# Attention and a squared-ReLU MLP on one core: earlier loads of the second batch, another conversion schedule, ReLU in place in PSUM

## Chip, core and metric

The kernel runs on one core of one Trainium2 chip. A core has TensorE (PE, with its weight loads as PEld), VectorE (DVE), ScalarE (ACT), GpSimd (POOL) and SyncE (SP), an on-chip memory SBUF, the matmul result memory PSUM, and DMA engines that move data between device memory and SBUF. The metric is the device time of one execution in microseconds (us); lower is better.

## The reference

```
kv  = einsum('bhsd,bhse->bhde', k, v)          # b=8, h=8, s=576, d=64
out = einsum('bhsd,bhde->bhse', q, kv)
out = out / sqrt(mean(out*out, -1) + 1e-6) * g_norm
x   = out as (b*s, h*d)                        # 4608 x 512
h   = x @ w_in                                 # 512 x 2048
r   = maximum(h, 0);  g = r * r
y   = g @ w_out                                # 2048 x 512
```

q, k, v and g_norm are float32. w_in and w_out come as float64 and are turned into float32 on the chip; the result is float32.

## The kernel before

The 4608 tokens are nine strips of 512. For each strip the kernel makes x from the attention, then the up products (x @ w_in, ReLU, square) and the down products (@ w_out). Strip 0 multiplies w_in plainly: 16 products (`up_first`, L741), each of a 128-column block of w_in with all 512 tokens, in four accumulating matmuls into one PSUM bank of 512 columns. Its down products, and the later strips, use sums and differences of blocks so that seven products do the work of eight; those of w_out are made on the chip and stored in device memory (`w_out`, `w_deep`).

**Opening.** Attention works on pairs of heads. For the pairs 0 to 3 of batch 0 a hand-written list of steps (L619 to L624) alternates the transposed query, k times v, the query product and the norm with the first conversions and up products. k and v of the last 64 tokens of each head (the "rests", k_rest and v_rest) are separate tiles; each pair's k times v ends with matmuls that read them (L408). The gain g_norm goes into the tile g_col, which scales x on its way out of PSUM (L545).

**Conversions.** The weights come as 32 pieces of 512 KiB (`raw`, 8 buffers): 16 of w_in and then 16 of w_out. A piece costs two ScalarE activations (L242, L245) and four VectorE instructions (L254 to L263). `convert(n)` (L319) does conversions, of two pieces each, until n are done; ScalarE always works two pieces ahead. Conversions 2 to 7 are of w_in, 8 to 11 of w_out's first half, 12 to 15 (`sums_out`, L300) of its second half, with four subtractions more each per piece; these also store their result (tile `wt`) to `w_out` with four DMAs each (L313). After each conversion the next pieces' loads are issued; each waits until the conversion of the piece eight before it has freed the buffer. The steps of strip 0 call `convert` by their number i: behind steps 0 to 3 up to 3, 4, 5 and 7, ahead of steps 4 to 10 up to 8, 9, 10, 10, 11, 12, 13, and behind steps 11 to 15 up to 13, 14, 15, 16, 16. So three conversions stand between the ReLU of product 3 and that of product 4.

**ReLU and square.** After each product of strip 0 ScalarE takes two halves of 256 tokens from PSUM: ReLU from PSUM into the tile `gt` in SBUF (L756), then the square in place there (L757). Four banks rotate, so product i waits for the ReLUs of product i-4.

**Queues.** Every engine executes its instructions in the order in which the program issues them. Nearly all loads and stores are issued by SyncE, in program order; a DMA that has to wait holds up all behind it. Eight semaphores tell of landed DMAs in rotation, so a DMA also waits until the one eight places before it (SyncE and ScalarE counted together) has landed. ScalarE issues the rests of batch 0 and g_col. The attention of batch 1 runs between the last products of strip 0 and in its down steps. Its loads are issued ahead of steps 4, 6 and 8 (pairs 0, 1, 2; `load_next`), 5 (rests) and 15 (the "last queries": the last 64 queries of each head of batches 0 and 1, tile q_rest); pair 3 and batch 2 follow from `key_value`.

**After the up steps.** VectorE makes `g_s` (sums of `gt`, L735), then sums of w_out's blocks into tiles `w_t` (`store_deep_sums`, L825). These tiles lie where the conversion buffers were, so the first waits for the last stores of `wt`. The norm's result x_n of the next strip comes behind them on VectorE, and TensorE's transposes of it (xt_ps, L570) stand between two down products. SyncE then stores the `w_t` sums (L837), stores converted blocks of w_out from w_in's tile to device memory (L863) and reads back weight blocks (`w_blk`, L804). `sums_in` (L287) then writes sums of w_in's blocks over the stored ones and so waits for those stores.

Of the kernel before, what the change touches and what calls it, by code (L numbers as in the profile page):

```python
# [14 lines left out]
AF = mybir.ActivationFunctionType  # L15
# [5 lines left out]
def kernel(  # L21
# [34 lines left out]
    nc = tc.nc  # L56
# [14 lines left out]
    TH = STRIP // 2  # L71
# [77 lines left out]
    def load_rest(b, eng):  # L149
        h = b % 2  # L150
        half = slice(REST * h, REST * (h + 1))
        for t, src in ((k_rest[half], k), (v_rest[half], v)):
            eng.dma_start(out=t, in_=src[b, :, C * P : S].rearrange("h s d -> s h d"))

    def load_q_rest(b, eng, one=None):
        h = b % 2
        if h == 0 and not one:
            q_rest[b // 2] = rest_pool.tile([P, H, D], FP32, name="q_rest", tag="q_rest")
        src = q[b, :, C * P : S]
        if b < Q_ON_PE:  # L160
            eng.dma_start(out=q_rest[b // 2][REST * h : REST * (h + 1)], in_=src.rearrange("h s d -> s h d"))
            return
        t = squares(q_rest[b // 2])
        for a in range(4) if one is None else (one,):
            hq, f = divmod(a * SQ, D)
            for kq in range(2):
                eng.dma_start(
                    out=t[ts(a, SQ), 2 * h + kq], in_=src[hq::2, ts(kq, SQ), f : f + SQ].rearrange("p i f -> i p f")
                )
# [4 lines left out]
    def load_next(q_eng=nc.sync, names="kvq"):  # L174
        u = next(to_load, None)
        if u is not None:
            load(*u, q_eng, names)
# [141 lines left out]
    def convert(n):  # L319
        while converted[0] < min(n, len(conversions)):  # L320
            fn, a = conversions[converted[0]]
            fn(a)
            converted[0] += 1
# [9 lines left out]
    nc.scalar.sqrt(one, one)  # L333

    load_next()
    load_rest(0, nc.scalar)
    for p in range(1, NP):
        load_next()
        load_piece()
# [2 lines left out]
    g_src = g_norm.rearrange("(d u) -> d u", u=1)  # L342
    for h in range(2):
        nc.scalar.dma_start(out=g_col[ts(h, D)], in_=g_src)


    qT, kvd, x_n, xt = {}, {}, {}, {}
# [319 lines left out]
    def attend(n):  # L667
        while slice_at[0] < min(n, len(slices)):
            fn, a = slices[slice_at[0]]
            fn(*a)  # L670
            slice_at[0] += 1
# [53 lines left out]
    def quarters(s, g):  # L725

        if (s, 11) not in gq:
            for q in (11, 12, 21, 22):
                gq[s, q] = g_pool.tile([P, FQ, TH], FP32, name="gt", tag="gt")
        return {q: gq[s, q][:, 2 * g : 2 * g + 2, :] for q in (11, 12, 21, 22)}  # L730

    def sum_g1(s, g):
        dest = quarters(s, g)
        s1 = gq[s, 1, g] = sum_pool.tile([P, 2, TH], FP32, name="g_s1", tag="sum")
        nc.vector.tensor_tensor(out=s1, in0=dest[12], in1=dest[22], op=ALU.add)  # L735
# [5 lines left out]
    def up_first(g, fh, i):  # L741

        tag = TAG_UP[2 * fh + i]
        if g == 0 and 2 * fh + i in first_sums:
            ps = first_sums.pop(2 * fh + i)
        else:
            ps = fpsum.tile([P, STRIP], FP32, name=f"ps_{tag}", tag="f")
            for kc in range(NP):
                nc.tensor.matmul(
                    ps, lhsT=w_in[:, kc % KH, g, kc // KH * 2 + fh, ts(i, P)], rhs=xt[0][:, :, kc, :],  # L750
                    start=kc == 0, stop=kc == NP - 1,
                )
        dest = quarters(0, g)
        for th in range(2):
            o = dest[(11, 12, 21, 22)[2 * fh + th]][:, i, :]
            nc.scalar.activation(o, ps[:, ts(th, TH)], AF.Relu)  # L756
            nc.scalar.activation(o, o, AF.Square)  # L757

    def up(s, g, p):
        open_bank(p)  # L760
# [406 lines left out]
    for s in range(N_STRIP):  # L1167
        attend(ready[s])
        if s == DEEP_UP - 1:
            while queried:  # L1170
                attend(slice_at[0] + 1)
            psums.close()
            fpsum = ctx.enter_context(tc.tile_pool(name="fpsum", bufs=5, space=bass.MemoryType.PSUM, reuse_waits="tile"))
            apsum = ctx.enter_context(tc.tile_pool(name="apsum", bufs=1, space=bass.MemoryType.PSUM, reuse_waits="tile"))
        if s >= DEEP_UP:
            steps = [(0.5, up_slot, (s, slot)) for slot in range(55)]
        elif s == 0:
            steps = [(2, up_first, (g, fh, i)) for g in range(NG) for fh in range(2) for i in range(2)]
        else:
            steps = [(1, up, (s, g, p)) for g in range(NG) for p in ORDER]  # L1180
        n_up = len(steps)
        if s < DEEP:

            steps += [(2, down, (s, p, i)) for p in (ORDER if s else (1, 2, 5, 6, 7, 3, 4)) for i in range(2)]
        else:
            steps += [(2, down_deep, (s, k, i)) for k in range(7) for i in range(2)]
        goal, begun = ready.get(s + 1, len(slices)), slice_at[0]
        if s >= DEEP_UP:
            goal = max(goal, min(ready[DEEP_UP] + (len(slices) - ready[DEEP_UP]) * (s - 1) // (N_STRIP - DEEP_UP - 1), len(slices)))
        total, done = sum(w for w, _, _ in steps), 0  # L1190
        for i, (w, fn, a) in enumerate(steps):
            if s == 0 and i < n_up:

                if 4 <= i < 11:
                    convert(5 + (3 * i + 2) // 4)
                if i in (4, 6, 8):
                    load_next()
                if i == 5:
                    load_rest(1, nc.sync)
                if i == 15:  # L1200
                    for b in range(2):
                        load_q_rest(b, nc.sync)
            elif s == 0 and i == n_up:
                convert(len(conversions))
                conv.close()

                stream_pool = ctx.enter_context(tc.tile_pool(name="stream", bufs=4, reuse_waits="tile"))
                sum_pool = ctx.enter_context(tc.tile_pool(name="sum", bufs=8, reuse_waits="tile"))
            if s == 0 and n_up <= i < n_up + 2:
                for g in range(2 * (i - n_up), 2 * (i - n_up) + 2):  # L1210
                    sum_g1(0, g)
            if s == 0 and n_up + 2 <= i < n_up + 4:
                for g in range(2 * (i - n_up) - 4, 2 * (i - n_up) - 2):
                    sum_g3(0, g)
            fn(*a)
            if s == 0 and i < 4:

                convert((3, 4, 5, 7)[i])
            done += w
            if s:  # L1220
                clock[0] += 3.2 if i >= n_up else 2.2 if s == DEEP else 1.2
                soon = tiles_due and tiles_due[0][2][0] // NT == s + 1
                if i == n_up + 10:
                    while tiles_due and tiles_due[0][2][0] // NT == s + 1:
                        _, f, a = tiles_due.popleft()
                        f(*a)
                elif not due(keys_due) and not (soon and due(tiles_due)):
                    least = 2.1 if s == DEEP else 4.5 if i < n_up else 3.3
                    if not (n_up * 2 // 3 < i < n_up + 3) and clock[0] >= dripped[0] + least:
                        dripped[0] = clock[0]  # L1230
                        drip(True)
                pace = 25 if s == DEEP else 36
                attend(begun + (goal - begun) * min(i + 1, pace) // pace)
                if s == DEEP and i == n_up - 3:
                    leaf_sums(s, 4)
                if s == 1 and i in range(2, 23, 3):
                    deep_sums_in((1, 6, 5, 4, 0, 2, 3)[i // 3])
                if s == 1 and i in (21, 22, 23, 25):
                    stream()
                continue  # L1240
            if i == n_up + 1:
                stream()
            if i == n_up + 8:
                load_next()
            if i == n_up + 9:
                load_rest(2, nc.sync)
                load_q_rest(2, nc.sync)
            if i - n_up in (7, 8, 9, 12):
                sums_in((7, 8, 9, 12).index(i - n_up))
            if i == n_up + 11:  # L1250
                sums_x(1)
            n = i + 1 - (n_up - 6)
            pairs, m = divmod(max(n - 2 * NP, 0), 3)
            attend(min(ready[0] + min(max(n, 0), 2 * NP) + (n >= 2 * NP) + 4 * pairs + (0, 2, 2)[m], goal))
            if 11 <= i < n_up:

                convert(5 + (3 * i + 2) // 4)
# [30 lines left out]
```

## Time and profile before

| what | us |
|---|---|
| three runs | 915.65, 916.85, 921.91 |
| median | 916.85 |
| profiled execution | 920.21 |
| its span, first to last instruction | 918.0 |
| TensorE busy | 888.5 (97%) |
| VectorE busy | 731.3 (80%) |
| ScalarE busy | 318.3 (35%) |
| GpSimd busy | 305.8 (33%) |

The profile is one execution. Its times count from the first instruction; "[2.12 <-ACT gt L756]" behind a row says that the engine stood idle for 2.12 us and that a ScalarE instruction of line 756 ended this. "SPq" and "ACTq" are issues of DMAs. The granted clock is the share of its full rate that TensorE was allowed. The page's row of the DMA engines by 40 slices and that of TensorE's clock read:

```
PEclk8999999999999999999999999999999999999999
DMA  9699898898989697979886987888657866785385
```

Up to about 92 us strip 0's opening and up products run, from there to 156 us its down products, and from then on the strips 1 to 8.

### The profile page before, as it was taken

The page shows a single profiled execution, that of the slowest core. Times are in us where ns is not written, and L with a number is a line of the kernel's source. Part 1 is how long each engine was busy: PE and PEld are TensorE (multiplying, and loading weights), DVE is VectorE, ACT ScalarE, POOL GpSimd, SP SyncE. Part 2 cuts the span into 40 slices and gives each one's busy share as a digit, 9 for nine tenths or more (in the row PEclk, how much of TensorE's full clock was granted, in tenths as well). Part 3 has the DMA queues.
Part 4 walks back from the last instruction along what each step waited for, and adds up shares of the span by engine and source line. Part 5 has one row for each costly group of instructions (what it writes and reads, how often), then busy time and mean ns, then how long its engine had stood idle before and what let it go on. Part 6 is the DMA issues. An engine that isn't in the chain of part 4 may idle for free.

```text
span 918.0 us, 20609 instructions
## 1 busy us (share of the span) xinstructions
PE 888.5 (97%) x8246; PEld 825.8 (90%) x8246; DVE 731.3 (80%) x1256; ACT 318.3 (35%) x638; POOL 305.8 (33%) x315
## 2 busy tenths in 40 slices
PE   7899998999999999999999999999999999999998
PEld 6434777889899999999999998999999999999998
DVE  2999878678958895789688967887689868975886
ACT  4797450321023701370128011720263027201710
POOL 0000000930057604560456044513362246234700
PEclk8999999999999999999999999999999999999999
DMA  9699898898989697979886987888657866785385
GB/s 266 222 292 307 252 341 269 247 293 309 285 265 239 229 341 238 252 238 337 268 220 217 333 286 206 241 283 305 207 163 256 304 220 186 255 304 177 124 310 184
DMA packets 172367, 235.71 MB, mean 257 GB/s; under 512 B 83568, under 2 KB 137328, under 8 KB 163824
## 3 DMA queue, kind: packets, MB, share of 16 engines
q1 hardware_dynamic: 171056, 234.14, 80.0%
q8 instruction: 65, 1.06, 0.5%
q10 hardware_dynamic: 1216, 0.26, 0.2%
q14 instruction: 30, 0.25, 0.1%
HBM read 197.66 MB, written 36.70 MB: 255 GB/s over the span
## 4 chain that ended last, share of the span: by engine, by line
PE 72%; DVE 11%; DMA 9%; ACT 3%; issue 2%; SPq 2%; DVEq 0%; ACTq 0%
PE ps_B L929 20%; PE ps_A L1117 16%; PE ps_A L929 15%; PE ps_B L1117 8%; PE ps_C L1117 4%; PE ps_A L708 4%; DMA q<-in_q_dram 2%; PE kv_ps L408 2%; PE x_ps L442 1%; PE ps_B L708 1%; DMA w_out<-w_in 1%; DMA w_blk<-w_out 1%; DVE w_c L260 1%; DVE w_t L280 1%; DVE o_sb L944 1%
## 5 line engine op out<-in xcount | busy, mean ns | idle before, releaser
L929 PE MATMUL ps_B<-w_blk,g_s 128*128 128x128 f32 x1024 | 126.2, 275 | 0.0
L929 PEld LDWEIGHTS ps_B<-w_blk,g_s 128*128 128x128 f32 x1024 | 120.0, 192 | 0.2
L1117 PE MATMUL ps_A<-x_l,w_in 128*128 128x128 f32 x784 | 104.1, 276 | 0.0
L929 PE MATMUL ps_B<-w_blk,gt 128*128 128x128 f32 x768 | 97.5, 275 | 2.0 <-DMA w_blk<-w_out 1.1
L280 POOL TENSOR_TENSOR x_l<-xT 128x256 f32<-128x256 f32 x21 | 16.1, 768 | 247.7 <-PE ps_A L929 247.7
L1117 PEld LDWEIGHTS ps_A<-x_l,w_in 128*128 128x128 f32 x784 | 95.4, 192 | 0.5 <-DVE gt L1129 0.2
L929 PEld LDWEIGHTS ps_B<-w_blk,gt 128*128 128x128 f32 x768 | 91.5, 192 | 2.4 <-issue 1.3
L929 PE MATMUL ps_A<-w_blk,g_s 128*128 128x128 f32 x768 | 93.6, 275 | 0.0
L929 PEld LDWEIGHTS ps_A<-w_blk,g_s 128*128 128x128 f32 x768 | 89.6, 192 | 0.0
L1129 POOL TENSOR_TENSOR snap<-snap,gt 128x512 f32<-128x512 f32 x35 | 46.5, 1330 | 123.2 <-ACT snap L1134 53.4
L1134 ACT COPY snap<-ps_A 128x512 f32<-128x512 f32 x63 | 36.6, 582 | 132.6 <-PE ps_A L1117 123.0
L944 DVE TENSOR_TENSOR o_sb<-o_sb,ps_B 128x256 f32<-128x256 f32 (+1 forms) x128 | 49.5, 387 | 35.9 <-ACT o_sb L945 28.5
L1067 ACT ACTIVATE gt<-gt 128x512 f32<-128x512 f32 x112 | 69.7, 622 | 18.1 <-DVE gt L1129 18.0
L929 PE MATMUL ps_A<-w_blk,gt 128*128 128x128 f32 x576 | 72.3, 275 | 1.3 <-DMA w_blk<-w_deep 1.3
L1068 ACT ACTIVATE gt<-gt 128x512 f32<-128x512 f32 x112 | 70.6, 631 | 3.6
L929 PEld LDWEIGHTS ps_A<-w_blk,gt 128*128 128x128 f32 x576 | 68.2, 192 | 1.5 <-DMA w_blk<-w_deep 1.5
L1027 POOL TENSOR_TENSOR w_i<-w_in 128x512 f32<-128x512 f32 x7 | 9.8, 1396 | 159.3 <-ACT sq L451 159.3
L1129 POOL TENSOR_TENSOR gt<-gt,snap 128x512 f32<-128x512 f32 x42 | 52.5, 1275 | 24.8 <-DVE snap L1129 24.7
L280 DVE TENSOR_TENSOR gt<-gt 128x2048 f32<-128x2048 f32 (+1 forms) x29 | 59.7, 2063 | 0.0
L945 ACT COPY o_sb<-ps_A 128x128 f32<-128x128 f32 x24 | 6.4, 265 | 147.3 <-PE ps_A L929 147.3
L1117 PE MATMUL ps_A<-x_l,w_blk 128*128 128x128 f32 x392 | 52.3, 276 | 1.4 <-issue 1.2
L1117 PE MATMUL ps_B<-x_l,w_blk 128*128 128x128 f32 x392 | 52.0, 276 | 0.0
(174 smaller groups left out, 1818.7 us busy)
## 6 DMA issues: line engine op xcount, KB each, us to landing
w_blk<-w_deep SPq DMA_DIRECT2D x56, 1024.0 KB, 6.7
w_blk<-w_out SPq DMA_DIRECT2D x56, 768.0 KB, 5.9
w_blk<-w_in_deep SPq DMA_DIRECT2D x49, 768.0 KB, 5.2
raw<-in_moe_w_in_dram SPq DMA_DIRECT2D x16, 512.0 KB, 5.8
raw<-in_moe_w_out_dram SPq DMA_DIRECT2D x16, 512.0 KB, 6.0
k<-in_k_dram SPq DMA_DIRECT2D x29, 256.0 KB, 4.8
v<-in_v_dram SPq DMA_DIRECT2D x29, 256.0 KB, 5.0
x_d<-x_q SPq DMA_DIRECT2D x27, 256.0 KB, 5.1
```

The lines of the kernel that those rows point to most:

```text
L260: yield nc.vector.scalar_tensor_tensor(out=ci, in0=high, scalar=-(2**30), in1=ci, op0=ALU.bitwise_and, op1=ALU.bitwise_or)
L280: eng.tensor_tensor(out=out, in0=a, in1=b, op=ALU.subtract)
L408: nc.tensor.matmul(ps[ts(h, D), i], lhsT=a, rhs=w, start=c == 0, stop=c == C)
L708: nc.tensor.matmul(bank[BANK[p]][:, i, :], lhsT=lhsT(k), rhs=rhs(k), start=p in (1, 5, 2) and i == 0 and k == 0, stop=k == n - 1, skip_gro ...
L929: nc.tensor.matmul(chain[c][x][:, i, :], lhsT=a[:, f, :], rhs=w[:, f, :], start=x not in opened[c] and f == 0, stop=f == FQ // 2 - 1, skip ...
L944: add = lambda out, a, b: nc.vector.tensor_tensor(out=out, in0=a, in1=b, op=ALU.add)
L1027: nc.gpsimd.tensor_tensor(out=s1, in0=w_half(b, 0, 1), in1=w_half(b, 1, 1), op=ALU.add)
L1067: nc.scalar.activation(o, o, AF.Relu)
L1068: nc.scalar.activation(o, o, AF.Square)
L1117: nc.tensor.matmul(ps[:, i, :], lhsT=w, rhs=rhs, start=j in (1, 2, 5) and i == 0, stop=True, skip_group_check=True)
L1129: add = lambda eng, out, a, b: eng.tensor_tensor(out=out, in0=a, in1=b, op=ALU.add)
L1134: nc.scalar.copy(t, ps)
```

## The change

The rests of batch 0 are issued behind g_col, and behind all loads of the opening, on ScalarE's queue. In `up_first` one ReLU of 128x512 is done in place in PSUM, and the two squares read PSUM and write `gt`: three instructions for four. The conversions of strip 0 follow one per step: behind steps 0 to 3 up to 3, 4, 5 and 6, ahead of steps 4 to 10 up to 7, 8, 9, 10, 11, 12 and 13, and from step 11 on as before. Pairs 0 and 1 and the rests of batch 1 are issued ahead of step 0, pair 2 ahead of step 1, and the last queries ahead of step 2. TensorE, VectorE and GpSimd have the same instructions in the same order as before.

```diff
@@ -333,7 +333,6 @@
     load_next()
-    load_rest(0, nc.scalar)
     for p in range(1, NP):
         load_next()
         load_piece()
@@ -342,6 +341,7 @@
     for h in range(2):
         nc.scalar.dma_start(out=g_col[ts(h, D)], in_=g_src)
+    load_rest(0, nc.scalar)
@@ -751,10 +751,9 @@
         dest = quarters(0, g)
+        nc.scalar.activation(ps, ps, AF.Relu)
         for th in range(2):
-            o = dest[(11, 12, 21, 22)[2 * fh + th]][:, i, :]
-            nc.scalar.activation(o, ps[:, ts(th, TH)], AF.Relu)
-            nc.scalar.activation(o, o, AF.Square)
+            nc.scalar.activation(dest[(11, 12, 21, 22)[2 * fh + th]][:, i, :], ps[:, ts(th, TH)], AF.Square)
@@ -1192,12 +1191,14 @@
             if s == 0 and i < n_up:
                 if 4 <= i < 11:
-                    convert(5 + (3 * i + 2) // 4)
-                if i in (4, 6, 8):
+                    convert(3 + i)
+                if i == 0:
                     load_next()
-                if i == 5:
                     load_rest(1, nc.sync)
-                if i == 15:
+                    load_next()
+                if i == 1:
+                    load_next()
+                if i == 2:
                     for b in range(2):
                         load_q_rest(b, nc.sync)
@@ -1215,7 +1216,7 @@
             fn(*a)
             if s == 0 and i < 4:
-                convert((3, 4, 5, 7)[i])
+                convert(3 + i)
```

## The prediction

> **What bounds the kernel now.** The page's first parts put TensorE at 97% of the span, so only what keeps TensorE waiting can be won. I listed TensorE's idle gaps in order of time: two thirds of them lie before 150 us, the stretch which the change touches. TensorE's timeline there (start, duration, engine, line, operation, and in brackets the idle time before it and what ended it):
>
> ```profile
> 57.66 5.40 PE L749 MATMUL ps_A<-xT,w_in 128*128 128x512 f32 x8 [2.12 <-ACT gt L756]
> ...
> 106.83 0.63 PE L392 MATMUL tr_ps<-ident,q_rest 128*128 128x128 f32 x4 [1.04 <-DMA q_rest<-in_q_dram]
> ...
> 115.38 1.32 PE L570 MATMUL xt_ps<-ident,x_n 128*128 128x128 f32 x8 [1.01 <-DVE x_n L510]
> ...
> 137.38 7.17 PE L708 MATMUL ps_B<-w_blk,gt 128*128 128x256 f32 x32 [0.88 <-DMA w_blk<-w_out]
> 147.82 8.80 PE L708 MATMUL ps_A<-w_blk,gt 128*128 128x256 f32 x32 [3.27 <-DVE o_sb L878]
> ```
>
> The first two gaps are what the change aims at; the last is the largest. A gap counts only if TensorE is not made to wait again later, so next comes the chain of waits, read backwards from 147.82 (start, duration, what):
>
> ```profile
> 101.02 4.84 DMA w_out<-wt
> ...
> 105.99 0.70 DVE w_t L280
> ...
> 129.40 11.16 DMA w_out<-w_in
> ...
> 147.82 2.50 PE ps_A L708 x5
> ```
>
> The chain into 147.82 does not pass through the gaps at 57.66 or 106.83. It runs: VectorE's conversions, the last store of converted weights (101.02), VectorE's sums, a DMA of 11.16 us, VectorE again, TensorE. VectorE's timeline shows why the conversions are its head:
>
> ```profile
> 93.50 0.43 DVE L254 TENSOR_SCALAR w_c<-w_c 128x512 f32<-128x512 f32 x1 [0.30 <-ACT w_c L242]
> ...
> 105.99 0.69 DVE L280 TENSOR_TENSOR w_t<-w_in 128x512 f32<-128x512 f32 x1 [3.89 <-DMA w_out<-wt]
> ...
> 140.68 1.29 DVE L280 TENSOR_TENSOR w_in<-w_in 128x512 f32<-128x512 f32 x2 [8.01 <-DMA w_out<-w_in]
> ```
>
> From 40.3 to 102.1 VectorE has one idle gap, the 0.30. Last, the table by stretch (busy us of each engine, granted clock, share and GB/s of the DMA engines):
>
> ```profile
> 20.00:38.00 18.00, 15.39 (x76) 8.64 (x77) 16.39 (x41) 11.03 (x25) 0.00 (x0) 1.00 0.73 261
> 38.00:55.00 17.00, 17.00 (x41) 7.41 (x39) 16.07 (x35) 16.62 (x35) 0.00 (x0) 1.00 0.77 241
> 55.00:78.00 23.00, 20.89 (x66) 9.16 (x64) 23.00 (x51) 22.56 (x51) 0.00 (x0) 0.93 1.05 301
> 105.00:108.60 3.60, 2.56 (x15) 2.01 (x14) 2.58 (x5) 0.00 (x0) 0.00 (x0) 1.00 0.04 9
> 108.60:148.00 39.40, 34.21 (x220) 28.52 (x219) 30.38 (x55) 12.88 (x15) 0.00 (x0) 1.00 0.97 324
> ```
>
> The DMA engines have room before 55, none from 55 to 105, stand still for 3.6 us while they wait for VectorE, and are then full until 148. So the stage from 105.99 to 147.82 moves as a block with the instant 105.99. The question is how much earlier that instant comes.
>
> **The change, part by part.** All sums are against the profiled execution: 918.0 us span in 920.21 us; the median of the three runs shown is 916.85, so I take differences over to the median.
>
> *One conversion per product.* Two conversions behind product 3 and one ahead of product 4 keep ScalarE from 49.39 to 56.5 off the ReLU that frees product 4's bank. This costs TensorE the 2.12 idle, and then 5.40 instead of the usual 3.60 us, at a granted clock of 0.50 from 59 to 62: 3.9 us. Afterwards two conversions stand there instead of three, and ScalarE is 2.25 us (38.15 to 40.40) earlier, so the gap goes. But VectorE takes 3.75 us per conversion (43.40, 47.23, 50.98, 54.73) without a break, in the same order after the change. I cost the 3.9 us at nothing at the end: TensorE comes early to the transposes at 115.38, where it waits for x_n, which VectorE makes after 105.99. That idle grows from 1.0 to about 4.5 us. The page "TensorE: Matmul & The Clock Gate" of the Trainium skill (section "What's actually happening") has the clock fall after at least one idle window of about 3.4 us; here it fell after 2.12 us of idle, but not after 1.04. By that rule the removed gap is worth only 2.1 us to TensorE; as nothing of it reaches the end, the sum stays.
>
> The longer idle at 115 will probably halve the clock for one stretch, by the 1.8 us that 57.66 shows. Cover: the two gaps behind it, 0.88 and 3.27. Without that cover it would cost 1.8.
>
> *ReLU in PSUM.* 32 ReLUs and 32 squares of 128x256 become 16 ReLUs of 128x512 and 32 squares. Four old ones take 1.45 us (36.70 to 38.15). A 128x512 activation out of PSUM takes 0.60 (L451). No row writes 128x512 into PSUM from ScalarE; the nearest, the roots of 128x16, take 0.18 to 0.19 into PSUM and 0.20 to 0.22 into SBUF, so I take 0.60, with 0.57 and 0.64 as ends. The first square must wait for it (0.04 issue), then two at 0.32 spacing: 1.28, a saving of 0.17 (0.1 to 0.25). The bank is held 1.28 instead of 1.09 us; with four banks this binds nowhere, as ScalarE needs 2.25 + 1.28 = 3.53 a step, below VectorE's 3.75. On the chain this counts once, at 38.15, where VectorE waits for ScalarE: **-0.2**.
>
> *Loads of the second batch.* Three pairs (768 KiB each), the rests and the last queries (256 KiB each) are 2.88 MB, at the 320 GB/s of 60 to 80 us about 9 us of DMA, moved from 59 to 103 into 20 to 51. On SP's queue the first pair passes pieces 8 to 23, the rests 8 to 25, the second pair 8 to 27, the third 14 to 27, and the last queries pass pieces 16 to 31, all stores of wt and two later pairs. A DMA also waits for the one eight places before it to land. Piece 8, issued at 23.96 because its buffer came free then, will go out at about 31.6 and land near 36; ScalarE wants it at 41.9. Pieces 16 and 17 land near 53.5 instead of 53.1, and VectorE wants them at 58.5, less 2.3 for ScalarE: 2.7 us to spare. I cost the delay at nothing; this cover is the rival below. Gained: the 5.00 us that ScalarE waits for piece 30 (91.50) go, and with them VectorE's **-0.3** (0 to -0.3). The gap of 1.04 goes too, into the same wait at 115.
>
> *The last store.* Eight stores of wt end the conversions. Seven land 2.75 to 3.33 us after issue, the last, with q_rest's small pieces issued right behind it, 4.84. Now q_rest is long there and the queue empty: I take 3.2, so **-1.6** (0, if it was not q_rest, to -2.1).
>
> *Rests behind g_col.* On ScalarE's queue the two g_col loads now go first; v_rest, which was issued at 1.67 and landed at 7.76, now waits for the second half of q of pair 0 to land (6.34 before; it may be 4.6, being no longer behind k_rest). Behind it on ScalarE stands the copy of qT (8.04), which until now stood behind g_col's wait at 7.50. v_rest then lands between 8.4 (issue 4.6 plus k_rest's 3.79) and 12.4 (6.34 plus its own 6.09). TensorE wants it at 9.61, when k and v of pair 0 have been multiplied, and these land up to 1.0 us sooner without the rests among them. The whole opening moves with it: -1.0 to +2.8; I take **-0.4**, as a queue of its own serves v_rest fast.
>
> Sum: -0.4 - 0.2 - 0.3 - 1.6 = **-2.5 us**, span 915.5, execution 917.7, median **914.4**. Ends: all low -3.75, all high +2.7, thus 913.1 to 919.5; if the 3.27 us gap at 147.82 falls across two clock windows, TensorE also keeps the 1.7 us that it loses there (8.80 against 7.07): 911.4.
>
> **The rivals.** *TensorE sets the end after all (0.15).* If the full DMA stage shrinks as well, the gaps come out: 3.9 + 0.4 + 0.5 + 1.0 + 1.0 + 0.9 + 3.3 + 1.7 = 12.7 us at most. For it: 97% busy. Against it: 0.97 of the DMA engines from 108.6, with an unchanged list of transfers. Between 2.5 and 12.7: about 909.
>
> *Nothing moves (0.17).* Late rests eat the other terms, or the last store takes 4.84 again: 916 to 918.
>
> *The early loads starve the conversions (0.15): slower.* One place: SP's queue between piece 7 (landed 28.35) and piece 17 (wanted at 56.2). 10 pieces of 0.524 MB and 2.88 MB are 8.1 MB in 27.9 us: 291 GB/s. It decides below that. For it: the stretches 20 to 55 moved 241 to 261. Against it: they did so at a share of 0.73 to 0.77. At 241 the pieces come 33.7 us after 28.35, 5.8 late, which VectorE hands on in full: 916.85 + 5.8 - 2.5 = 920. Below 200 it would pass 926. The page "DMA: Bandwidth & Descriptors" of the skill (Specifications) asks 512 bytes for line rate, and q and the rests come in 256 byte pieces; the row is kinder: 128 KiB of q land 0.5 us apart, 256 KiB of k or v 0.7. By the rule q and the rests (1.3 MB) might cost double, as an estimate 4 us more; piece 17 would land at 57.6, 1.4 us late, and the sum would be -1.1.
>
> **How the numbers follow.** The forecast has 0.53, with 911.4 to 919.5. What a measurement of this kernel tells from no change is 1%, 907.7 to 926. Faster than that needs most of the first rival, half of it: 0.07. Slower needs the third at its worst, half of it: 0.07. Within: 0.86. The range 909 to 919.5 leaves out the outer halves of these two rivals and little else.
>
> **What would show it.** Right: no gap above 0.5 before product 8; no wait for q_rest; idle before xt_ps near 115 grown to 4 us or more; VectorE's wait for w_out<-wt ended near 103.5; the 8 us wait for w_out<-w_in and the gap of about 3 before TensorE still there, 2 to 3 us earlier. Step by step: L754 at 0.57 to 0.64 us; piece 8 landed near 36; v_rest's landing against TensorE's first product with it. Wrong: VectorE idle between 40 and 92, which means starved conversions; or a DMA wait well below 11 us at 129, and then TensorE gains more than I allow.

## The result, and the profile after

| | before | changed |
|---|---|---|
| median of 22 runs | 916.99 us | 916.39 us |
| lowest to highest | 913.8 to 922.2 us, and one run of 2360.1 | 911.9 to 920.4 us |
| profiled execution (span) | 920.21 (918.0) | 918.22 (916.2) |

The run of 2360.1 us counts in the median, not in the ratio. The ratio is 0.9988, 95% interval 0.997 to 1.0006: the kernel is 1.1 us faster by the estimate, and no change is inside the interval. The forecast was 2.5 us less, at 914.4; the rival "nothing moves" had 916 to 918.

TensorE's timeline of the changed kernel, at the places that the prediction listed (start, duration, engine, line, operation, idle before and what ended it):

```profile
57.51 3.60 PE L749 MATMUL ps_A<-xT,w_in 128*128 128x512 f32 x8
...
78.89 1.11 PE L384 MATMUL t_ps<-ident,q 128*128 128x128 f32 x4 [2.54 <-ACT qT L386]
...
118.63 1.32 PE L570 MATMUL xt_ps<-ident,x_n 128*128 128x128 f32 x8 [3.13 <-DVE x_n L510]
...
149.31 7.17 PE L708 MATMUL ps_A<-w_blk,gt 128*128 128x256 f32 x32 [1.27 <-DVE o_sb L877]
```

The ninth product (57.51) no longer waits and runs at its usual 3.60; the wait for q_rest is gone too. But the time is handed back 21 us later, ahead of the second transposes of batch 1 (78.89): the PSUM tile that they need is freed by ScalarE's copy L386, which stands in ScalarE's queue behind ReLUs and conversions. Before, the same place had a gap of 0.40:

```profile
69.76 0.60 PE L384 MATMUL t_ps<-ident,q 128*128 128x128 f32 x4
...
78.70 0.66 PE L384 MATMUL t_ps<-ident,q 128*128 128x128 f32 x4 [0.40 <-ACT qT L386]
```

The chain of waits (start, duration, what) has the same links as before, only later:

```profile
104.31 4.80 DMA w_out<-wt
...
109.24 0.70 DVE w_t L280
...
131.44 10.61 DMA w_out<-w_in
```

The last store takes 4.80 us, as before (4.84), although no q_rest is issued behind it any more. VectorE's timeline:

```profile
96.13 0.43 DVE L254 TENSOR_SCALAR w_c<-w_c 128x512 f32<-128x512 f32 x1 [0.94 <-ACT w_c L242]
...
109.24 0.69 DVE L280 TENSOR_TENSOR w_t<-w_in 128x512 f32<-128x512 f32 x1 [4.52 <-DMA w_out<-wt]
...
142.17 1.29 DVE L280 TENSOR_TENSOR w_in<-w_in 128x512 f32<-128x512 f32 x2 [4.91 <-DMA w_out<-w_in]
```

In this execution w_t starts 3.25 us later than before, not 2.5 earlier, and still the span is 1.7 us shorter. Of the 3.25, 2.1 are there from the opening. When the last w_out<-w_in lands, near 141, they have shrunk to 1.5 (its stage took 32.8 us instead of 34.6), and when strip 1's up products begin near 156 both kernels are level (156.45 before, 156.32 now), as the gap ahead of them is 1.27 instead of 3.27. Strip 2's up products start 0.6 us earlier than before; the rest of the 1.7 comes behind that. The table by stretch (busy us of PE, PEld, DVE, ACT, POOL; granted clock; DMA share; GB/s) shows the loads where they were moved to:

```profile
20.00:38.00 18.00, 14.86 (x93) 8.86 (x92) 15.16 (x40) 11.77 (x26) 0.00 (x0) 0.98 1.02 312
38.00:55.00 17.00, 17.00 (x41) 7.48 (x40) 16.30 (x36) 15.52 (x32) 0.00 (x0) 1.00 0.90 255
55.00:78.00 23.00, 21.35 (x71) 9.51 (x69) 23.00 (x50) 22.39 (x47) 0.00 (x0) 1.00 0.82 273
```

The DMA share rose from 0.73 to 1.02 between 20 and 38, where 312 GB/s were moved instead of 261, and fell from 1.05 to 0.82 between 55 and 78. VectorE is busy for all 23.00 us of the last stretch: the early loads do not starve the conversions.

### The profile page after: what moved, and what is told of

It is laid out like the page before. It is cut to its first block, busy times and chain, and to the rows that moved or that the text cites. A ratio compares the mean times of both kernels' runs of the same rounds, so it can differ in the third digit from the quotient of the medians.

```text
span 916.2 us, 20585 instructions
## 1 busy us (share of the span) xinstructions
PE 890.1 (97%) x8246; PEld 828.9 (90%) x8246; DVE 732.8 (80%) x1256; ACT 315.0 (34%) x622; POOL 306.0 (33%) x315
## 4 chain that ended last, share of the span: by engine, by line
PE 76%; DVE 12%; DMA 6%; issue 2%; ACT 2%; SPq 1%; DVEq 0%; ACTq 0%
PE ps_B L928 21%; PE ps_A L928 16%; PE ps_A L1116 16%; PE ps_B L1116 8%; PE ps_C L1116 4%; PE ps_A L708 3%; PE kv_ps L408 3%; PE x_ps L442 2%; PE ps_B L708 1%; DMA w_out<-w_in 1%; DVE w_c L260 1%; DVE w_t L280 1%; DVE gt L1128 1%; DVE ms L459 1%; DMA raw<-in_moe_w_out_dram 1%
## 5 line engine op out<-in xcount | busy, mean ns | idle before, releaser
L943 DVE TENSOR_TENSOR o_sb<-o_sb,ps_B 128x256 f32<-128x256 f32 (+1 forms) x128 | 49.5, 387 | 34.6 <-ACT o_sb L944 27.3
```

What stands on the lines that cost most here:

```text
L943: add = lambda out, a, b: nc.vector.tensor_tensor(out=out, in0=a, in1=b, op=ALU.add)
```

## The experiments

Two executions of one kernel differ by more than these parts: the runs of each kernel spread over 4 to 10 us. So verdicts rest on ratios to the kernel before, and the traces say by what road. Some instants of the profiles, in us from the first instruction ("packet" is explained below):

| | before | whole | whole again (f4) | a1 | a1 again (f3) | f1 | f2 | b3 | b4 | a3 |
|---|---|---|---|---|---|---|---|---|---|---|
| VectorE's fifth L260 | 36.13 | 38.26 | 35.96 | 37.12 | 33.17 | 35.76 | 36.20 | 35.90 | 37.11 | 44.89 |
| last conversion ends | 99.61 | 102.24 | 99.07 | 100.88 | 95.88 | 98.85 | 98.91 | 99.13 | 100.16 | 107.83 |
| last store takes | 4.84 | 4.80 | 4.53 | 4.80 | 4.54 | 3.82 | 3.57 | 3.80 | 3.43 | 4.75 |
| packet starts after its issue by | 2.08 | 1.68 | 2.11 | 1.66 | 1.89 | 5.12 | 4.00 | 3.95 | 2.72 | 1.57 |
| w_t starts | 105.99 | 109.24 | 105.14 | 107.53 | 101.96 | 104.84 | 104.01 | 104.69 | 105.13 | 114.39 |
| last w_out<-w_in lands | 140.56 | 142.05 | 139.59 | 140.53 | 136.72 | 137.64 | 137.35 | 137.81 | 138.51 | 147.67 |
| strip 2's up products start | 258.75 | 258.18 | 258.55 | 256.01 | 252.87 | 252.49 | 255.16 | 255.29 | 255.75 | 266.86 |

**The place of the rests.** The changed kernel with the rests in front again (a1), the kernel before with only the rests moved (a2), and the changed kernel with the rests later still (a3):

```diff
 a1, to the changed kernel
     load_next()
+    load_rest(0, nc.scalar)
     for p in range(1, NP):
...
-    load_rest(0, nc.scalar)
 a2, to the kernel before: the two lines the other way round
 a3, to the changed kernel
         load_piece()
+        if p == 2:
+            load_rest(0, nc.sync)
...
-    load_rest(0, nc.scalar)
```

> The changed kernel with the rests of batch 0 back in their old place, ahead of g_col. Theory (the opening lost 2.1 us and handed them on, and so took back what the other parts gave): TensorE's wait of 1.8 us for v_rest near 10.5 is gone, VectorE's conversion 2 starts near 34.8 instead of 36.9, the end comes 2 us earlier, about 914.3, ratio to before 0.997. Rival (the stage of full DMA engines from 109 on, or TensorE, absorbs what comes late from the opening): the same 34.8, but 916 to 917, ratio 0.999 to 1.000.

> The kernel before with nothing changed but the rests of batch 0, behind g_col. Theory: v_rest lands near 10.5, conversion 2 starts near 36.9, the end comes 2 us later, about 919, ratio 1.002. Rival: the same opening, but 916 to 917.5, ratio 1.000.

> The changed kernel with the rests of batch 0 still later: on SyncE's queue, behind pair 2 and piece 1. They land near 17, TensorE's first product with them waits to 17, conversion 2 starts near 43, 6 us later than in the changed kernel. Theory: the end follows by 5 to 6.5, about 922, ratio to before 1.0055. Rival: the later stages absorb half or more of it, 916.5 to 919.5.

Measured: a1 0.9974 (0.9952 to 0.9996), a2 1.0003 (0.9983 to 1.0023), a3 1.0067 (1.0042 to 1.0092). In a3, where line numbers are one higher, TensorE waits for the rests in this row of its timeline:

```profile
18.44 0.48 PE L409 MATMUL kv_ps<-v_rest,k_rest 64*64 64x64 f32 x4 [11.05 <-DMA v_rest<-in_v_dram]
```

Against the whole change, VectorE's fifth L260 comes 6.6 us later, the last conversion ends 5.6 later, w_t starts 5.2 later, and the median is 7.6 us higher (923.96 against 916.39). So what the opening loses comes out at the end in full. The trace has it in VectorE's conversions all the way, but TensorE carries it as well (the first of its products of 3.60 us starts at 46.97 instead of 40.34), so this run alone does not say which of the two hands it on. Whether the rests behind g_col lose anything at all, these three could not settle; the four cells below come back to it.

**One part alone.** The kernel before with the conversion schedule alone (b3), with the loads alone (b4), with the ReLU in PSUM alone (c1):

```diff
 b3
-                    convert(5 + (3 * i + 2) // 4)
+                    convert(3 + i)
...
-                convert((3, 4, 5, 7)[i])
+                convert(3 + i)
 b4: the lines of load_next, load_rest(1, ...) and load_q_rest of the change
 c1: the lines of up_first of the change
```

> The kernel before with the new conversion schedule alone. Theory (VectorE's conversions lead to the end, TensorE's time before 75 us is cover): the gap of 2.12 us at 57.66 and the half clock behind it go and TensorE is some 2 us early at the first transposes near 68, but a gap of 1.5 to 3 us stands before the second transposes near 78, since ScalarE gets to their copies no sooner; the last conversion ends within 0.5 us of the 99.6 us before, w_t starts within 0.5 us of 105.99, and the idle before xt_ps grows from 1.0 to 2 to 4.5 us. Ratio 0.998 to 1.002. Rival (TensorE sets the end): the 3.9 us come out, 913 us, ratio 0.996, with no new gap.

> The kernel before with the early loads of batch 1 and of the last queries alone. Theory now (after the profile of the changed kernel): the gap at 57.66 stays, the one for q_rest near 107 goes, the last store of wt still takes 4 us or more with no q_rest behind it, and w_t starts 0 to 2 us later than 105.99 because the loads for batch 2 and the stores of the last conversions come together at 93 to 100; ratio 0.999 to 1.003. The prediction's reason: no wait before the last conversion, the last store lands 3.2 us after its issue, w_t starts near 104, ratio 0.998.

> The kernel before with the ReLU of 128x512 in place in PSUM alone, one look. Theory: L754 takes 0.57 to 0.63 us, a product's ReLU and squares 1.2 instead of 1.45 us, and VectorE is 0.2 to 0.3 us earlier from 45 us on, through to w_t, whatever the opening does. Rival: the bank that is held longer (until the last square) makes TensorE wait for a ReLU, with gaps over 0.3 us before L749 that are not in the kernel before.

Measured: b3 0.996 (0.9939 to 0.9981), b4 0.9981 (0.9959 to 1.0002); c1 has one execution, 918.41 us, and serves for its trace. TensorE's timeline in b3:

```profile
65.75 0.60 PE L384 MATMUL t_ps<-ident,q 128*128 128x128 f32 x4
...
79.04 0.66 PE L384 MATMUL t_ps<-ident,q 128*128 128x128 f32 x4 [4.75 <-ACT qT L386]
```

The first transposes come at 65.75 instead of 69.76, so TensorE is 4.0 us ahead, but the second ones at 79.04 instead of 78.70: all of it is given back, in a gap that was 0.40. That is the theory's mechanism. Its other numbers are not: the idle before xt_ps, which was to grow, is gone, w_t starts 1.3 us earlier, and b3 is faster by 0.4%, which is what the rival expected, without the rival's mechanism. The next fences show a part of the road. How much of the 0.4% is the schedule's stays open: f1 below, the same schedule together with the ReLU in PSUM, has 0.9976, and the two intervals overlap.

In b4 the two numbers of the prediction appear: no wait before the last conversion, last store in 3.43 us. But not for the prediction's reason, since in b3 the store takes 3.80 with q_rest right behind it. What differs is in the rows of the DMA queues between the issue of the last store and its landing (queue and kind, packets, MB, share of 16 engines), first the kernel before:

```profile
q1 hardware_dynamic: 3006, 1.24, 91.7%
q8 instruction: 1, 0.02, 1.5%
```

then b3:

```profile
q1 hardware_dynamic: 2912, 1.24, 115.2%
```

In GB/s, in 40 slices of that time, the changed kernel (where no q_rest follows) and b3 read:

```profile
GB/s 345 341 336 353 349 341 341 345 358 345 328 328 332 485 319 319 336 315 320 332 319 324 345 336 192 43 38 34 21 21 21 21 21 26 21 21 21 0 0 0
GB/s 345 345 350 345 345 345 345 340 345 350 345 345 345 350 340 345 345 345 345 350 345 345 340 351 340 345 345 334 340 340 326 313 280 299 294 286 251 199 226 251
```

One packet of the kind "instruction", about 1 us long on one DMA engine, falls into this time in the kernel before and in the changed one, and not in b3. In the changed kernel only some 21 to 43 GB/s move for 1.4 us ahead of the landing, about what one of 16 engines carries (an estimate: 340 / 16 is 21); so one engine, it seems, finishes late, by about the packet's length. The 14 profiled executions of this study agree: where the packet starts 1.6 to 2.2 us after the last store's issue (nine of them), that store takes 4.3 to 4.8 us; where it starts 2.7 us or more after it (b4, e1, b3, f2, f1), the store takes 3.0 to 3.8. In six of the nine the store before the last is slow too (4.2 to 4.9 us). In all 14 the packet starts during one and the same TensorE product (ps_C<-w_in,gt). A TensorE that is later against VectorE, as behind b3's gap of 4.75, would so get it out of the store's way. That the packet causes the delay was not tried by an edit; it is read from this coincidence and from the tail of the one engine. What q_rest adds by itself is small: 3.57 to 3.82 with it (f1, f2, b3) and 3.02 and 3.43 without (e1, b4), all with the packet out of the way.

In c1 the ReLU L754 takes 0.58 to 0.62 us, and VectorE gains 0.3 us between its fifth L260 and 42 us, as in all kernels with this ReLU; no new gap stands before L749.

**Gains that are lost after strip 0.** a1 with pair 0 of batch 2 loaded later (a4), and a4 with no loads of later queries in strip 1's down steps (e1):

```diff
 a4, to a1
-                if b == 1 and p < 2:
+                if b == 1 and p < 1:
                     load_next()
...
             if i == n_up + 8:
                 load_next()
+                load_next()
 e1, to a4
-                    if not (n_up * 2 // 3 < i < n_up + 3) and clock[0] >= dripped[0] + least:
+                    if not (n_up * 2 // 3 < i < n_up + 3) and clock[0] >= dripped[0] + least and not (s == 1 and i >= n_up):
```

> As the first of these, with one more edit: pair 0 of batch 2 is loaded together with its pair 1 in the down steps of strip 0, not ahead of the last stores of wt. Theory: SyncE issues these stores as soon as VectorE has made them, the last lands near 103 to 104.5 instead of 109.1, VectorE's first w_t starts there, and the end is 2 to 3 us below the first of these: about 912, ratio 0.9945. Rival (what bounds is TensorE or the full DMA stage behind it): as the first of these, within 1 us.

> The kernel that had lost its lead between 240 and 253 us (rests in front, first pair of batch 2 loaded later), now with no loads of later queries in the down steps of strip 1: they follow in strip 2. Theory (a second stage with full DMA engines, 205 to 250 us, takes back what arrives early: gaps of 0.52 and 1.85 us before w_blk<-w_deep and 1.7 us of half clock): without these 12 small loads (3.6 us of DMA at 16 engines' rate) the gaps fall by 1 to 2.4 us together and the half clock goes; span 911 to 913, ratio 0.993 to 0.996. Rival (the blocks of w_deep come late for another reason, such as their buffers): the gaps stay, ratio 0.998 as without this edit, or higher when the moved loads make VectorE wait near 290.

Measured: a4 0.9987 (0.9967 to 1.0008), e1 1.0013 (0.9998 to 1.0029); both miss the ratios of their theories. In a4's profile w_t starts at 103.96, but TensorE then waits in strip 1's down steps:

```profile
239.69 1.16 PE L928 MATMUL ps_B<-w_blk,gt 128*128 128x128 f32 x8 [0.52 <-DMA w_blk<-w_deep]
...
248.05 1.16 PE L928 MATMUL ps_A<-w_blk,gt 128*128 128x128 f32 x8 [1.85 <-DMA w_blk<-w_deep]
```

The table by stretch has the DMA engines at 0.96 from 205 to 252 in a4 (0.97 in the changed kernel):

```profile
205.00:252.00 47.00, 44.39 (x354) 42.97 (x353) 38.89 (x58) 3.14 (x8) 3.31 (x4) 0.97 0.96 315
```

This is a second stage with full DMA engines, and by the theory it takes back part of what arrives early. e1 fits that: both gaps go (one of 0.56 us at 225 is new), and strip 2 begins at 254.03 instead of 256.93. It is one profile, though, and f1, which has these loads in their place, has no such gap either. But the queries that were held back are then late for VectorE, and TensorE waits for them:

```profile
269.22 0.34 PE L442 MATMUL x_ps<-kv_all,qT_rest 64*64 64x64 f32 x8 [4.15 <-DVE qT_rest L372]
```

The transfers can't be dropped; where they stand, one stage or another pays.

**Four cells.** By the first profiles I held that early loads and the new schedule get in each other's way: in the changed kernel the loads for batch 2 held SyncE until 98.86, the stores of the last conversions went out only from 98.96 on (96.04 before), and VectorE waited 0.94 instead of 0.30. To test this, loads early or as before, and rests in front or behind, all with the schedule and the ReLU of the change, on one chip:

```diff
 f1: b3 and c1 together        (loads as before, rests in front)
 f2: changed kernel, loads as before (rests behind g_col)
 f3: a1 again                  (early loads, rests in front)
 f4: changed kernel again      (early loads, rests behind g_col)
```

> One of four cells (loads of batch 1 early or as before; rests of batch 0 in front or behind g_col), all with one conversion per product and the ReLU in PSUM: here loads as before, rests in front. Theory (early loads and the earlier conversion schedule get in each other's way: the last pieces and the stores of the last conversions wait for eight landings): without the early loads w_t starts at 104 to 105 (105.99 in the kernel before), VectorE waits less than 0.4 us before the last conversion; ratio 0.995 to 0.997, best of the four. Rival (the loads do nothing; parts differ by chance of the run): ratio 0.997 to 0.9985 like the other three.

> Of the four cells: loads as before, rests behind g_col, that is the whole change without its early loads. Theory: w_t some 1 us later than in the cell with the rests in front, by what the opening loses, and 1 to 2 us earlier than in the whole change; ratio 0.996 to 0.998. Rival (the loads do nothing): the ratio of the whole change, 0.998 to 0.9995.

> Of the four cells: early loads, rests in front (the kernel a1 once more, for the comparison on one chip). Theory: 0.997 again, the wait before the last conversion 0.6 to 1 us and the first store of the last two conversions held until 97 or later. Rival (chance): anywhere from 0.996 to 0.9985, and in step with the cell with loads as before.

> Of the four cells: early loads, rests behind g_col, the whole change once more. Theory: 0.9985, 1 to 1.5 us above the cell with the rests in front, because the opening is later by that in most runs (second conversion's last step at 37 to 38.3 against 35.5 to 37.1). Rival (the opening's loss in the first profile was chance of its clock windows): the same as with the rests in front, second conversion at 35.5 to 37.

| ratio (95%) | rests in front | rests behind g_col |
|---|---|---|
| loads as before | f1 0.9976 (0.9955 to 0.9997) | f2 0.9991 (0.9969 to 1.0012) |
| early loads | f3 0.9975 (0.9955 to 0.9995) | f4 0.9988 (0.9963 to 1.0012) |

My theory falls. Beside the new schedule the early loads do nothing that shows in the time: the mean of f3's and f4's 24 runs is 0.6 us above that of f1's and f2's, with 1.25 for two standard errors. And the wait of 0.94 was chance: VectorE waits 0.29 in the same place in f4 and not at all in f3. What shows is the place of the rests: f2 and f4 are 1.3 us above f1 and f3 (two standard errors: 1.2). With the rests in front, the kernels are faster than the one before with intervals that end below 1: a1 and f3 at 0.9974 and 0.9975, f1 at 0.9976.

In the traces the early loads do show: they move TensorE's wait. First f1, with loads as before, then f4, with early loads:

```profile
80.36 1.11 PE L384 MATMUL t_ps<-ident,q 128*128 128x128 f32 x4 [6.51 <-DMA raw<-in_moe_w_out_dram]
```

```profile
76.58 0.66 PE L384 MATMUL t_ps<-ident,q 128*128 128x128 f32 x4 [2.25 <-ACT qT L386]
...
114.52 1.31 PE L570 MATMUL xt_ps<-ident,x_n 128*128 128x128 f32 x8 [2.21 <-DVE x_n L510]
```

All three kernels with the new schedule and the loads as before idle 4.75 to 6.51 us ahead of the second transposes (b3, f2, f1; ScalarE itself waits 0.8 to 3.8 us for pieces of weights between 56 and 80) and less than 0.3 before xt_ps. All with the new schedule and early loads idle 2.2 to 2.5 us there, and 1.9 to 3.1 before xt_ps or, in e1, 2.0 at 95. TensorE gives its lead back either way.

Why the first profile made the rests look worse (2.13 us) shows in TensorE's timeline of the opening, in the changed kernel, in its second execution (f4), and in f3:

```profile
10.52 0.43 PE L408 MATMUL kv_ps<-v_rest,k_rest 64*64 64x64 f32 x4 [1.81 <-DMA v_rest<-in_v_dram]
11.63 2.05 PE L520 MATMUL x_ps<-kv_all,qT 128*128 128x128 f32 x8 [0.67 <-ACT kv_all L412]
...
16.52 2.08 PE L520 MATMUL x_ps<-kv_all,qT 128*128 128x128 f32 x8 [0.53 <-ACT kv_all L412]
```

```profile
9.50 0.48 PE L408 MATMUL kv_ps<-v_rest,k_rest 64*64 64x64 f32 x4 [0.96 <-DMA v_rest<-in_v_dram]
10.65 2.05 PE L520 MATMUL x_ps<-kv_all,qT 128*128 128x128 f32 x8 [0.67 <-ACT kv_all L412]
...
15.31 1.16 PE L520 MATMUL x_ps<-kv_all,qT 128*128 128x128 f32 x8 [0.52 <-ACT kv_all L412]
```

```profile
8.58 0.33 PE L408 MATMUL kv_ps<-v_rest,k_rest 64*64 64x64 f32 x4
9.59 1.13 PE L520 MATMUL x_ps<-kv_all,qT 128*128 128x128 f32 x8 [0.68 <-ACT kv_all L412]
...
12.55 1.16 PE L520 MATMUL x_ps<-kv_all,qT 128*128 128x128 f32 x8 [0.53 <-ACT kv_all L412]
```

Of the first two query products (L520) both run at half rate in the first (2.05 and 2.08 for 1.16), one in the second, none in the third; the fifth L260 follows at 38.26, 35.96 and 33.17. That is chance of the execution: a1 is the same kernel as f3 and has both slow (37.12). The wait for v_rest itself, 1.81 and 0.96, is in every kernel with the rests behind g_col (1.55 in f2, 1.57 in a2) and in none with them in front. With one product slow, the fifth L260 comes at 35.96 in f4 and at 35.76 in f1, so that in the traces the move costs 0.2 to 1.1 us (38.26 less 37.12) at equal clock.

## Why the prediction was right, and where its steps failed

The number lies in the range, but the range (909 to 919.5) holds no change as well, and 916.39 is also inside the 916 to 918 of the rival "nothing moves". Both conditions of that rival came true: the last store took 4.80 again, and the late rests cost 1.3 us by the four cells. What held is what the range rests on: neither the 3.9 us taken from TensorE nor the 1.04 for q_rest came out of the whole change. b3's timeline shows the cover; a3 fits the first link, VectorE's conversions, without setting TensorE apart.

Of the signs named, the gap before product 8, the wait for q_rest, L754 and piece 8 came as forecast, and none of the signs of being wrong showed. Other signs failed: the idle before xt_ps was 3.13 and 2.21, not 4 or more; the wait for w_out<-wt ended at 109.24 and 105.14, not near 103.5; the 8 us wait and the gap of 3 were to come 2 to 3 us earlier and came 1.0 earlier in f4, and later and smaller in the first profile. The low ends of the terms add up to -3.65, not -3.75. Of the terms:

- *One conversion per product, 3.9 us at nothing.* The gap went (57.51). The cover was named too late: not the idle before xt_ps alone, but first the second transposes of batch 1: 2.54 with half clock behind it, 2.25 in f4, 4.75 in b3. The half clock behind the idle at xt_ps came in the first profile (5.31 us for a product of 3.62) and not in f4; in the first profile the gaps behind it covered it, as forecast (0.88 went, 3.27 became 1.27). And "nothing" was too little: b3 is 0.4% faster (0.2 to 0.6%), f1 with the ReLU added 0.2% (0 to 0.45%). One piece of it is the last store, 1.0 us shorter in b3. The rest I can't place: its stage from w_t to the last w_out<-w_in took 33.1 us instead of 34.6, but the whole change has 32.8 and 34.5 in its two executions, so that one profile does not say whose the 1.5 us are. With the loads as before, the three kernels with the new schedule have 32.8 to 33.3 (f1, b3, f2) and the three with the old one 34.6 to 34.8 (before, c1, a2): a hint, not a proof.
- *ReLU in PSUM, -0.2.* Right in kind: 0.57 to 0.63 for L754, and -0.3 on VectorE, a little more than the 0.1 to 0.25 of the ends.
- *Early loads, -0.3, and their rival.* Piece 8 landed at 36.19 (forecast 36). Pieces 16 and 17 landed at 56.95 and 58.19, not 53.5, and even so VectorE did not wait between 42 and 94. But ScalarE's wait for piece 30, which was to go, did not: it grew from 5.00 to 7.79 us (7.12 in f4), as the piece landed at 93.96 (91.42 before). The 0.3 before the last conversion varies from 0 to 0.97 between two executions of one kernel (f3 and a1), so these profiles can't show the term.
- *The last store, -1.6.* This step's reason failed: q_rest behind it was not what slowed it. With q_rest gone it took 4.80; with it there, 3.80 in b3. The size was about right where the packet is out of the way (3.43 in b4). In the whole change it is not, so the term came to nothing.
- *Rests behind g_col, -0.4.* Right in mechanism, wrong in size and sign. v_rest was issued when the second half of q landed, at 5.14 and in f4 at 4.68, as the low end had it (4.6). But I let it land 3.79 us later, by k_rest's row, since "a queue of its own serves v_rest fast"; it took 5.33 and 4.77. v_rest's own 6.09 was the nearer row. Measured cost: 1.3 us, two standard errors 1.2, inside the ends of the term (-1.0 to +2.8).
- *"The stage moves as a block with the instant 105.99."* Within 2 us: its length is 32.8 to 34.8 over the kernels, and differs by 1.6 between two executions of the changed kernel (33.0 and 34.8 in a1 and f3). The 8 us wait is 4.91 in the first profile, 7.90 in f4; the gap before TensorE 1.27 and 3.23.

So -0.2 stood and the forecast's -1.6 became 0; the conversions' 0 became a gain and the rests' -0.4 a loss of about 1.3. Alone, rests, schedule and loads give +0.3, -3.7 and -1.7 us (ratio times 917), together -1.1; but each has some 2 us of uncertainty to either side. From the four cells the parts do add up: -2.2 for schedule and ReLU (f1), +1.3 for the rests and +0.6 for the loads are -0.3, within the noise of the whole. That the total came near the forecast is luck in part: errors that cancel.

## What to carry to other kernels

When a gap on a busy engine is removed, look along its queue for the next place where it meets the slower engine: here ScalarE's copy, 21 us on, took it all back, long before the place that the chain of waits showed. Where the stages of one kernel vary by 2 to 4 us between executions, a single profile before and after can't size terms of 1 us; run each part alone, and the same kernel twice, before a story is built on a difference. And a transfer that is moved off a busy queue needs a look at what it then waits for, not only at what it passes.

## What was not expected of the hardware

- The half rate of the opening depends on the execution: 33.17 to 37.12 for the same instruction of the same kernel (f3 and a1). Later, one and the same stall had half rate behind it or not: 2.54 us of idle at 78.89 was followed by transposes of 1.11 us, 2.25 us at the same place in f4 by 0.66. 2.33 us before xt_ps in f3 was followed by a window at 0.50, 2.80 in a1 was not, and neither was 3.13 us ahead of a down product in a3 (154.93). The page "TensorE: Matmul & The Clock Gate" of the Trainium skill (What's actually happening) has the clock fall after at least one idle window of about 3.4 us; here it fell after 2.3 and stayed after 3.1, so the length of the gap alone does not tell. The half-rate stretches in the records last 3.41 us or multiples of it.
- The last store of 256 KiB landed in 3.0 to 3.8 us in five executions, and in 4.3 to 4.8 in the nine in which a packet of instructions started on the DMA queues 1.6 to 2.2 us after its issue. No edit moved the packet alone.
- Of a DMA stage of some 33 to 35 us with the same transfers, two executions differ by 1.6 to 1.8 us; what decides it stays open.
